# An attention stage whose SyncE transfers keep the order in which they are written, with the weights' and the noise's loads moved to later slots

## The chip, the cores and the metric

The kernel runs on one core of a Trainium2 chip. The metric is the device time of one execution, in microseconds (us). Five engines work side by side, each through its own list of instructions in order: PE (TensorE, matmuls), DVE (VectorE), ACT (ScalarE), POOL (GpSimd) and SP (SyncE, which here only issues DMAs). An engine waits where the next instruction of its list is not ready, and everything behind it waits too.

## The reference

Three stages in a row, all in float32. Attention in two steps over 4 batches, 8 heads, 576 tokens and head dimension 64: 32 packed queries per head read the keys and values, and then the tokens' own queries read the packed result. Then a mixture of 8 experts over the 2304 tokens (512 features) with noisy top-2 routing. Then a dense gated layer (2048 hidden).

```python
p_packed = sm_attn(p, k, v)                     # 32 packed rows per head
out = sm_attn(q, p_packed, p_packed)            # -> x, 2304 x 512
noisy = x @ w_gate + log1p(exp(x @ w_noise)) * noise
top2 = argpartition(-noisy, 2)[:, :2]           # softmax over the two -> top2_w
for e in range(8): out[mask] += top2_w * (relu(x[mask] @ w1[e]) @ w2[e])
h = x @ w_in;  y = (h * sigmoid(h)) @ w_out
```

## The kernel before, in words

The program has three stages: attention with routing (the first 120 us or so), the experts, and the dense layer. The change touches the first.

**Attention by slots.** A Python loop over 16 slots emits the work. Eight units of `packed` (a batch and four heads each) turn and multiply keys and values (`kp`, `s`, `a`, `pp`); ten units of `unpacked` (two tiles of 128 tokens, or one) do the second step. `START1` and `START2` say at which slot a unit starts, `LAG1` and `LAG2` when its phases follow. A unit of `unpacked` makes scores `s` (PE), a softmax over them (`mx` and `sd`: DVE, an exponential on ACT, the last multiplication on POOL, L446), turns the result (`a2p` on PE, copied to `a2T` by ACT), multiplies with `ppBD` (PE, `xp`, L460), and copies each tile to `xr` (ACT, two halves), from where SP writes it to `xs` in memory (L467). `xr` has two buffers. The last 16 columns of `xp` are the routing logits `lg`.

**Weights of expert 0.** Eight tiles of weights are loaded in the attention stage. Each takes a buffer `raw` (three of them): four DMAs of 128 KB for each of the first four tiles (L137), one DMA of 512 KB for each of the last four (L140). Two ticks of the slot loop later the tile is split into a high part (`wa0h` ... `wa7h`, one ACT activation, L115) and a low part (`wa0l` ... `wa7l`, four POOL subtractions of 256 columns, L119). The weight tiles use the same memory as keys and values: weight tile `i` waits until unit `i` of `packed` is done with its own.

**Routing.** `route` is a long chain of small DVE operations (`rt_*`). It runs once for the first 11 tiles (r0) and once for the last 7 (r1). r0 ends in a list of tokens `idx0`, by which POOL fetches two tiles `xg` (L196) for the first block of expert 0 (`hps`, `acc` with `xha`). r1 ends in `idx`, by which the rest is fetched; the second block is the first that reads `xhb`. r1 needs the last logits, so it needs the last units of `unpacked`.

**What sets the order.** A scheduler of the framework orders each engine's list by an estimate of times, free to move an instruction ahead of others that were emitted earlier; instructions given to `tc.keep_in_program_order` keep their emitted order among themselves. In the kernel before, the DMAs of the attention stage are not given to it.

Of the kernel before, what the change touches and what calls it, by code (L numbers as in the profile page):

```python
# [7 lines left out]
F32 = mybir.dt.float32  # L8
# [11 lines left out]
P = 128  # L20
B, H, S, D, PK = 4, 8, 576, 64, 32
# [4 lines left out]
REST = S - 4 * P  # L26
# [18 lines left out]
def body(ctx: ExitStack, tc: tile.TileContext, q, k, v, p, wg, wn, noise, w1, w2, w_in, w_out, out):  # L45
    nc = tc.nc
# [76 lines left out]
    def tick():  # L123

        later.append(None)
        while later.count(None) > M["delay"]:
            fn = later.pop(0)
            if fn:
                fn()

    def load(dst, src, c, eng=V, runs=False):

        hi, lo = dst
        raw = raws.tile([P, 1024], F32, name="raw", tag="raw")
# [100 lines left out]
    def expert_block(e, j0, n, x):  # L235
        ws = W[e % 2]
        acc = [None]

        def step2(f, h):
            if f == 0:  # L240
                acc[0] = [M["a"].tile([P, DM], F32, name="acc", tag="acc") for _ in range(n)]
            second(acc[0], h, ws, f, 7)
            if f == 7:
                for j, y in enumerate(acc[0]):
                    ysb = M["s"].tile([P, DM], F32, name="ysb", tag="ysb", bufs=3)
                    cp(A if j % 2 else V, ysb, y)
                    i = j0 + j
                    r0 = (e * TA + i if i < TA else E * TA + e * TB + i - TA) * P
                    nc.sync.dma_start(ys[r0:r0 + P, :], ysb)
        for f in range(8):  # L250
            ps = first(ws, x, f, n * P)
            h = relu_split(ps, n * P)
            flush(M["lag"])
            pend.append(lambda f=f, h=h: step2(f, h))
            yield f


    with ExitStack() as ax:
# [6 lines left out]
        sk = ph.enter_context(tc.tile_pool(name="attk", bufs=2))  # L265
# [143 lines left out]
        def unpacked(t, n, lg):  # L409
# [45 lines left out]
            for i in range(n):  # L455
                xr = sb.tile([P, 512], F32, name="xr")
                for g in range(2):
                    xp = pMx.tile([P, 272], F32, name="xp", tag="m")
                    for b, sl in parts:
                        T.matmul(xp[sl], aT[:, 2 * i + g, sl], ppBD[b, g], start=True, stop=True)  # L460
                    if g:
                        V.tensor_tensor(lg[:, i, :], xp[:, 256:272], lg[:, i, :], op=OP.add)
                    else:
                        V.tensor_copy(lg[:, i, :], xp[:, 256:272])
                    cp(A, runs(xr)[:, 2 * g:2 * g + 2], xp[:, 0:256].rearrange("p (b a j) -> p b a j", b=2, a=4))
                r0 = (t + i) * P
# [149 lines left out]
        for slot in range(START2[-1] + LAG2[-1] + 1):  # L616
# [339 lines left out]
```

## Time and profile before

| | us |
|---|---|
| median of 3 runs | 995.24 (993.43 to 997.77) |
| the profiled execution | 991.13 |
| its span, first to last instruction | 989.3 |
| PE busy in the span | 957.0 (97%) |
| DVE, ACT, POOL busy | 447.4, 346.4, 313.4 |

The span is that of the profiled execution; 1.8 us of its time lie outside the span. PE is busy 97% of it, so what PE lacks is in the first 150 us: the page's 40 slices (24.7 us each) show PE at 6, 9, 8, 9 and 7 tenths in the first five slices and at 9 or more from the sixth to the last but one. Below, a time at the start of a row is in us from the span's start.

### The profile page before, as it was taken

To read this page: it belongs to the slowest core of one execution; us is meant where nothing else is said; L and a number is where in the kernel's file an instruction comes from. 1 tells how busy PE (TensorE), PEld (TensorE's weight loads), DVE (VectorE), ACT (ScalarE), POOL (GpSimd) and SP (SyncE) were. 2 spreads that over 40 slices of the span, in tenths; PEclk is the share of its full clock that TensorE was granted. 3 is DMA by queue.
4 is the path that set the end of the run, shared out by engine and by line. 5 is a ranking of instruction groups with operands and counts; after the bars stand their busy time and mean duration, and the time that the engine had idled before them with its cause. 6 is when DMAs were issued, how large, how long until landed. Compare 5 with 4: busy or idle time off the path is not lost.

```text
span 989.3 us, 14385 instructions
## 1 busy us (share of the span) xinstructions
PE 957.0 (97%) x5584; PEld 821.0 (83%) x5584; DVE 447.4 (45%) x871; ACT 346.4 (35%) x631; POOL 313.4 (32%) x345
## 2 busy tenths in 40 slices
PE   6989799999999999999999999999999999999996
PEld 4767589899999999998999988888888888888884
DVE  4537763666767576766634557222122221111111
ACT  3567322433434343433323343322222222222221
POOL 2166214343525243443200136333323322222221
PEclk9989899999999999999999999999999999999998
DMA  9994324576757676566623454111011110001001
GB/s 243 249 270 161 107 65 125 188 231 202 231 167 227 188 235 199 189 226 207 188 64 117 149 194 136 54 28 37 22 53 33 32 43 1 1 1 43 0 1 46
DMA packets 82298, 122.49 MB, mean 124 GB/s; under 512 B 16432, under 2 KB 49200, under 8 KB 82224
## 3 DMA queue, kind: packets, MB, share of 16 engines
q1 hardware_dynamic: 74704, 101.58, 32.6%
q0 software_dynamic: 7520, 19.93, 7.0%
q8 instruction: 46, 0.75, 0.3%
q14 instruction: 28, 0.23, 0.1%
HBM read 93.17 MB, written 28.31 MB: 123 GB/s over the span
## 4 chain that ended last, share of the span: by engine, by line
PE 90%; DVE 4%; DMA 3%; ACT 1%; SPq 1%; issue 1%; ACTq 0%
PE hps L208 14%; PE hps L210 14%; PE hps L209 14%; PE acc L219 14%; PE acc L218 14%; PE acc L220 14%; PE xp L460 1%; PE tps L157 1%; PE s L429 1%; PE s L362 1%; DMA vm<-in_v_dram 1%; DMA km<-in_k_dram 1%; DVE rt_oa L534 1%; PE kp L351 0%; DMA raw<-wf_out 0%
## 5 line engine op out<-in xcount | busy, mean ns | idle before, releaser
L176 POOL DMA_INDIRECT xg<-xs,idx x120 | 127.0, 1059 | 195.1 <-DVE xturn L185 147.6
L750 POOL TENSOR_TENSOR gl<-sg,gh 128x512 fp32r<-128x512 f32 (+1 forms) x80 | 95.4, 1194 | 253.5 <-ACT gh L749 237.9
L231 ACT ACTIVATE hh<-hps 128x384 fp32r<-128x384 f32 (+1 forms) x128 | 56.0, 438 | 260.5 <-PE hps L210 256.8
L746 DVE TENSOR_TENSOR sg<-hps,sg 128x512 f32<-128x512 f32 (+1 forms) x80 | 50.7, 634 | 196.2 <-ACT sg L745 196.0
L232 DVE SCALAR_TENSOR_TENSOR hl<-hps,hh 128x384 fp32r<-128x384 f32 (+1 forms) x128 | 62.4, 488 | 122.0 <-ACT hh L231 121.3
L745 ACT ACTIVATE sg<-hps 128x512 f32<-128x512 f32 (+1 forms) x80 | 44.2, 553 | 189.5 <-PE hps L210 189.2
L749 ACT ACTIVATE gh<-sg 128x512 fp32r<-128x512 f32 (+1 forms) x80 | 47.1, 589 | 79.3 <-DVE sg L746 79.1
L736 POOL DMA_INDIRECT y<-ys,slots x36 | 36.7, 1019 | 110.9 <-DVE hl L232 72.4
L739 DVE TENSOR_SCALAR y<-y,gates 128x512 f32<-128x512 f32 x18 | 10.9, 607 | 37.9 <-DMA y<-ys,slots 37.9
L740 DVE SCALAR_TENSOR_TENSOR y<-y,gates,y 128x512 f32<-128x512 f32 x18 | 15.7, 871 | 25.1 <-DMA y<-ys,slots 25.0
L460 PE MATMUL xp<-ppBD,a2T 128*128 128x272 f32 (+1 forms) x80 | 23.5, 433 | 1.6 <-ACT xr L51 0.8
L185 DVE STREAM_TRANSPOSE xturn<-xg 128x512 f32<-128x512 f32 x30 | 21.2, 706 | 3.7 <-DMA wf_in<-t 2.5
L689 DVE SCALAR_TENSOR_TENSOR t<-raw,t 128x512 int32<-128x512 int32 x32 | 22.2, 693 | 0.9
L690 DVE SCALAR_TENSOR_TENSOR t<-raw,t 128x512 int32<-128x512 int32 x32 | 22.1, 691 | 0.9
L196 POOL DMA_INDIRECT xg<-xs,idx x10 | 9.7, 969 | 40.3 <-DVE idx_f L555 19.5
L686 ACT ACTIVATE t<-raw 128x512 f32<-128x512 f32 x32 | 21.2, 662 | 0.1
L208 PE MATMUL hps<-xha,wa3h 128*128 128x256 f32 (+1 forms) x56 | 17.7, 316 | 1.8 <-DVE sg L746 1.8
L160 DVE TENSOR_TENSOR xla<-tps,xha 128x512 fp32r<-128x512 f32 x14 | 9.6, 690 | 21.1 <-ACT xha L159 21.1
L53 DVE COPY ysb<-acc 128x512 f32<-128x512 f32 x24 | 16.4, 682 | 4.9 <-PE acc L220 4.8
L429 PE MATMUL s<-ppT,qT 128*128 128x64 f32 x128 | 17.9, 291 | 0.0
L208 PE MATMUL hps<-xha,wa0h 128*128 128x256 f32 (+1 forms) x56 | 17.6, 314 | 0.2 <-ACT xha L159 0.2
L208 PE MATMUL hps<-xha,wa2h 128*128 128x256 f32 (+1 forms) x56 | 17.7, 316 | 0.1
(450 smaller groups left out, 2976.4 us busy)
## 6 DMA issues: line engine op xcount, KB each, us to landing
raw<-in_moe_w_dram SPq DMA_DIRECT2D x56, 512.0 KB, 4.0
ys<-ysb SPq DMA_DIRECT2D x40, 256.0 KB, 3.7
raw<-in_moe_w_in_dram SPq DMA_DIRECT2D x16, 512.0 KB, 4.3
raw<-in_moe_w_out_dram SPq DMA_DIRECT2D x16, 512.0 KB, 4.1
xs<-xr SPq DMA_DIRECT2D x18, 256.0 KB, 2.1
km<-in_k_dram SPq DMA_DIRECT2D x8, 512.0 KB, 7.6
vm<-in_v_dram SPq DMA_DIRECT2D x8, 512.0 KB, 7.6
qm<-in_q_dram SPq DMA_DIRECT2D x8, 512.0 KB, 7.1
```

Of the source, the lines that this page charges most:

```text
L176: G.indirect_dma_start(out=xg[:, g * P:(g + 1) * P], out_offset=None, in_=xs[:, :].rearrange("n (a f) -> (n a) f", a=4), in_offset=bass.In ...
L208: T.matmul(ps, wh[:, c, s], xh[:, c, :n], start=c == 0, stop=False)
L209: T.matmul(ps, wh[:, c, s], xl[:, c, :n], start=False, stop=False)
L210: T.matmul(ps, wl[:, c, s], xh[:, c, :n], start=False, stop=c == 3)
L218: T.matmul(y, hh[:, s], wh[:, f % 2, :], start=f == 0, stop=False)
L219: T.matmul(y, hh[:, s], wl[:, f % 2, :], start=False, stop=False)
L220: T.matmul(y, hl[:, s], wh[:, f % 2, :], start=False, stop=f == last)
L231: A.activation(hh, ps, AF.Relu)
L232: V.scalar_tensor_tensor(hl, ps, 0.0, hh.bitcast(F32), op0=OP.max, op1=OP.subtract)
L746: V.tensor_tensor(sg, ps, sg, op=OP.mult)
L749: A.activation(gh, sg, AF.Copy)
L750: G.tensor_tensor(gl, sg, gh.bitcast(F32), op=OP.subtract)
```

## The change

All SyncE DMAs of the attention stage go through a helper `dma` that gives them to `tc.keep_in_program_order` as long as `M["queue"]` is set; it is cleared after the slot loop. Expert 0's weight tiles are loaded at slots 6 to 13, one a slot (before: slots 4, 5, 6, 7, 8, 8, 11 and 12), and the noise at slot 8 (before: 4). The 64-row rests of keys and values (`kr`, `vr`) have four buffers each (before three), and batch 3's value rests are loaded after its mains. The packed queries `pd` lie in one of the three `raw` buffers.

```diff
-WLOAD = 4
+WSLOT = (6, 7, 8, 9, 10, 11, 12, 13)
+NOISE = 8
...
+    def dma(dst, src):
+        ins = nc.sync.dma_start(dst, src)
+        if M["queue"]:
+            tc.keep_in_program_order(ins)
...
-                nc.sync.dma_start(raw[32 * b:32 * b + 32].rearrange("j (a f) -> j a f", a=4),
+                dma(raw[32 * b:32 * b + 32].rearrange("j (a f) -> j a f", a=4),
...
-            r = sk.tile([REST, 4, 64], F32, name=f"{nm}r", bufs=3)
+            r = sk.tile([REST, 4, 64], F32, name=f"{nm}r", bufs=4)
...
-        pd = sk.tile([P, 9, 64], F32, name="pd", bufs=1)
+        pd = raws.tile([P, 1024], F32, name="pd", tag="raw")[:, 0:576].rearrange("p (c d) -> p c d", d=64)
...
-                nc.sync.dma_start(xs[r0:r0 + P, :], xr)
+                dma(xs[r0:r0 + P, :], xr)
...
-            if slot == 4:
+            if slot == NOISE:
                 load_noise()
...
-            for i, s0 in enumerate(START1):
-                if slot == s0 + WLOAD:
+            for i, s0 in enumerate(WSLOT):
+                if slot == s0:
                     W[0].append(weight_tile(wa, "wa", i))
...
+        M["queue"] = False
```

The scheduler orders the other engines anew. Three places follow, each before and after. A number behind a name tells one tensor from another of the same name; the numbers of the two programs differ.

SP, where the first token tiles are written to `xs`, before: noise and weights stand between and ahead of the last queries (`qm`) and of the first `xs`.

```order
L302 DMA nzt<-in_moe_noise_dram 64x8
L137 DMA raw<-in_moe_w_dram 32x4x256 x5
L288 DMA qm<-in_q_dram 128x4x256
L279 DMA vr<-in_v_dram 64x4x64
L279 DMA kr<-in_k_dram 64x4x64
...
L137 DMA raw<-in_moe_w_dram 32x4x256 x7
...
L288 DMA qm<-in_q_dram 128x4x256 x2
L137 DMA raw<-in_moe_w_dram 32x4x256
L467 DMA xs<-xr 128x512
```

SP, the same place after:

```order
L108 DMA qm<-in_q_dram 128x4x256 x2
L108 DMA qr<-in_q_dram 64x8x64
L108 DMA xs<-xr 128x512 x2
L108 DMA raw<-in_moe_w_dram 32x4x256 x4
...
L108 DMA nzt<-in_moe_noise_dram 128x32
L108 DMA nzt<-in_moe_noise_dram 64x8
...
L108 DMA xs<-xr 128x512 x4
L108 DMA raw<-in_moe_w_dram 32x4x256 x4
```

The last queries are now ahead of every weight; the first weight tile stands behind the second `xs`, the second behind the fourth; the eight noise loads follow, then four `xs`, the third weight tile, three `xs` and the fourth.

ACT, the first three splits of weights before (`wa0h` to `wa2h`):

```order
L115 ACTIVATE wa0h_638<-raw_640 128x1024
L51 ACTIVATE a1T_842<-ap_835 128x512
L51 ACTIVATE ppBD11_181<-wp_809 128x16
L51 ACTIVATE xr_815<-xp_816 128x2x4x32
L51 ACTIVATE a1T_875<-ap_868 128x512
L442 ACTIVATE sd2_912<-sd2_912 128x512
L51 ACTIVATE xr_815<-xp_820 128x2x4x32
L51 ACTIVATE xr_825<-xp_826 128x2x4x32
L115 ACTIVATE wa1h_782<-raw_784 128x1024
L51 ACTIVATE qT_937<-qp_938 128x512
L51 ACTIVATE xr_825<-xp_830 128x2x4x32
L115 ACTIVATE wa2h_957<-raw_959 128x1024
```

ACT after, from the fourth token tile (`xr_987`) to `wa1h`, and from the eighth (`xr_1110`) to `wa2h`:

```order
L52 ACTIVATE xr_987<-xp_992 128x2x4x32
L52 ACTIVATE a2T2_1078<-a2p_1073 128x512
L52 ACTIVATE qT_1140<-qp_1141 128x512
L52 ACTIVATE ppBD21_189<-wp_971 128x16
L52 ACTIVATE xr_1080<-xp_1081 128x2x4x32
L52 ACTIVATE xr_1080<-xp_1085 128x2x4x32
L52 ACTIVATE qT_1140<-qp_1147 128x512
L121 ACTIVATE wa1h_1051<-raw_1053 128x1024
...
L52 ACTIVATE xr_1110<-xp_1115 128x2x4x32
...
L52 ACTIVATE a1T_1402<-ap_1395 128x512
L121 ACTIVATE wa2h_1171<-raw_1173 128x1024
```

Six ACT instructions stand between `xr_987` and `wa1h`, and six between `xr_1110` and `wa2h`; between the eleventh token tile and `wa3h` there are eight (one row of them stands for two). `wa0h` no longer stands ahead of the two `a1T`.

POOL, at the end of the attention stage, before:

```order
L119 TENSOR_TENSOR wa5l_1200<-raw_1201,wa5h_1199 128x256 x4
...
L119 TENSOR_TENSOR wa6l_1522<-raw_1523,wa6h_1521 128x256 x4
L396 COPY ppBD30_193<-px_1278 32x64 x4
L119 TENSOR_TENSOR wa7l_1614<-raw_1615,wa7h_1613 128x256 x4
L396 COPY ppBD31_197<-px_1444 32x64 x4
L446 TENSOR_TENSOR sd2_1586<-sd2_1586,mx22_1584 128x512
L196 DMA xg_1755<-xs_69,idx0_102 128x512
L196 DMA xg_1757<-xs_69,idx0_102 128x512
L446 TENSOR_TENSOR sd2_1645<-sd2_1645,mx22_1643 128x512
L446 TENSOR_TENSOR sd1_1663<-sd1_1663,mx21_1661 128x256
L196 DMA xg_2013<-xs_69,idx_101 128x512
```

POOL at the same place after; `sd2_1567`, `sd2_1631` and `sd1_1649` are what `sd2_1586`, `sd2_1645` and `sd1_1663` were, the softmax of the last three units:

```order
L125 TENSOR_TENSOR wa2l_1172<-raw_1173,wa2h_1171 128x256 x4
L411 COPY ppBD30_193<-px_1253 32x64 x4
L125 TENSOR_TENSOR wa3l_1299<-raw_1300,wa3h_1298 128x256 x4
L411 COPY ppBD31_197<-px_1426 32x64 x4
L125 TENSOR_TENSOR wa4l_1434<-raw_1435,wa4h_1433 128x256 x4
L202 DMA xg_1755<-xs_69,idx0_102 128x512
L202 DMA xg_1757<-xs_69,idx0_102 128x512
L461 TENSOR_TENSOR sd2_1567<-sd2_1567,mx22_1565 128x512
L125 TENSOR_TENSOR wa5l_1503<-raw_1504,wa5h_1502 128x256 x4
L125 TENSOR_TENSOR wa6l_1600<-raw_1601,wa6h_1599 128x256 x4
L461 TENSOR_TENSOR sd2_1631<-sd2_1631,mx22_1629 128x512
L461 TENSOR_TENSOR sd1_1649<-sd1_1649,mx21_1647 128x256
```

Behind the two fetches `xg` now stand the softmax of unit 7, two splits and the softmax of units 8 and 9, where only the latter two stood; three splits (`wa2l` to `wa4l`) stand ahead of the fetches in the stretch of r0, where two stood (`wa6l`, `wa7l`).

## Rows read from the trace of the kernel before

**Rows 1.** Stretches: length, busy PE, PEld, DVE, ACT, POOL; granted clock, DMA share, GB/s.

```profile
50.00:62.00 12.00, 9.07 (x79) 7.52 (x78) 3.90 (x13) 6.54 (x12) 5.65 (x8) 0.72 1.09 262
62.00:84.00 22.00, 21.80 (x232) 16.47 (x230) 12.29 (x37) 17.86 (x41) 16.32 (x29) 1.00 0.84 250
...
104.00:120.00 16.00, 11.05 (x77) 7.51 (x78) 11.79 (x31) 5.76 (x14) 4.25 (x5) 0.79 0.25 76
120.00:149.00 29.00, 28.31 (x227) 23.29 (x225) 17.85 (x85) 7.79 (x20) 4.76 (x5) 1.00 0.23 73
149.00:989.00 840.00, 829.07 (x4261) 723.17 (x4260) 362.15 (x550) 274.15 (x461) 261.94 (x239) 1.00 0.36 114
```

**Rows 2.** PE in order of time, 48 to 63 us: start, length; idle before, releaser.

```profile
48.46 1.10 PE L429 MATMUL s<-ppT,qT 128*128 128x64 f32 x8
...
53.57 0.66 PE L377 MATMUL ap<-ident,a 128*128 128x128 f32 x4 [2.93 <-ACT a1T L51]
...
54.52 3.47 PE L429 MATMUL s<-ppT,qT 128*128 128x64 f32 x16
```

**Rows 3.** ACT in order of time, 48 to 63 us.

```profile
51.98 1.06 ACT L115 ACTIVATE wa0h<-raw 128x1024 fp32r<-128x1024 f32 x1 [3.29 <-DMA raw<-in_moe_w_dram]
...
58.55 1.06 ACT L115 ACTIVATE wa1h<-raw 128x1024 fp32r<-128x1024 f32 x1 [2.56 <-DMA raw<-in_moe_w_dram]
```

**Rows 4.** SP in order of time, 38 to 116 us: start and length of each issue.

```profile
38.66 1.48 SPq L300 DMA_DIRECT2D nzt<-in_moe_noise_dram  x1
...
46.88 0.47 SPq L302 DMA_DIRECT2D nzt<-in_moe_noise_dram  x1
47.39 2.49 SPq L137 DMA_DIRECT2D raw<-in_moe_w_dram  x5
...
59.63 0.37 SPq L467 DMA_DIRECT2D xs<-xr  x1
...
85.46 5.10 SPq L467 DMA_DIRECT2D xs<-xr  x4
```

**Rows 5.** DMA issues of the first 125 us: KB each, median us to landing.

```profile
xs<-xr SPq DMA_DIRECT2D x18, 256.0 KB, 2.1
...
raw<-in_moe_w_dram SPq DMA_DIRECT2D x24, 128.0 KB, 3.1
```

**Rows 6.** DVE in order of time, 86 to 126 us.

```profile
91.96 0.77 DVE L487 SCALAR_TENSOR_TENSOR rt_h<-rt_h,rt_w 128x88 f32<-128x88 f32 x1
92.76 0.66 DVE L488 TENSOR_TENSOR rt_sp<-rt_sp,rt_h 128x88 f32<-128x88 f32 x1
93.45 0.67 DVE L490 COPY_PREDICATED rt_sp<-rt_big,rt_sa 128x88 f32<-128x88 int32 x1
94.16 0.25 DVE L492 TENSOR_TENSOR rt_ny<-rt_sp,nzt 128x88 f32<-128x88 f32 x1
...
98.42 0.68 DVE L439 TENSOR_REDUCE mx<-s 128x16 f32<-128x512 f32 x1
...
99.55 0.68 DVE L441 TENSOR_TENSOR sd<-s,mx 128x512 f32<-128x512 f32 x1
...
101.03 0.67 DVE L443 TENSOR_REDUCE mx<-sd 128x16 f32<-128x512 f32 x1
...
105.52 3.28 DVE L534 TENSOR_TENSOR rt_oa<-iota_lo,rt_lo 128x768 f16<-128x768 f16 x4
```

**Rows 7.** POOL in order of time, 50 to 136 us.

```profile
91.14 2.86 POOL L119 TENSOR_TENSOR wa6l<-raw,wa6h 128x256 fp32r<-128x256 f32 x4 [5.03 <-PE pp L388]
...
110.79 1.15 POOL L196 DMA_INDIRECT xg<-xs,idx  x1 [6.32 <-PE s L436]
112.25 0.95 POOL L196 DMA_INDIRECT xg<-xs,idx  x1 [0.31 <-DVE lg L464]
113.22 1.05 POOL L446 TENSOR_TENSOR sd<-sd,mx 128x512 f32<-128x512 f32 x1
114.72 0.62 POOL L446 TENSOR_TENSOR sd<-sd,mx 128x256 f32<-128x256 f32 x1 [0.44 <-DVE lg L464]
```

More of the change, by code (lines that the diff above doesn't have):

```diff
@@ L102, in body @@
     few = const.tile([P, E], F32)
-    M = {"pin": False, "w": 384, "hb": 3}
+    M = {"pin": False, "w": 384, "hb": 3, "queue": True}
+    def dma(dst, src):
+        ins = nc.sync.dma_start(dst, src)
+        if M["queue"]:
+            tc.keep_in_program_order(ins)
     def pin(ins):
@@ L136, in load @@
             for b in range(4):
-                nc.sync.dma_start(raw[32 * b:32 * b + 32].rearrange("j (a f) -> j a f", a=4),
+                dma(raw[32 * b:32 * b + 32].rearrange("j (a f) -> j a f", a=4),
                                   src[b * P:(b + 1) * P].rearrange("(a j) f -> j a f", a=4))
         else:
-            nc.sync.dma_start(raw.rearrange("p (c f) -> p c f", c=c), src.rearrange("(c p) f -> p c f", p=P))
+            dma(raw.rearrange("p (c f) -> p c f", c=c), src.rearrange("(c p) f -> p c f", p=P))
         later.append(lambda: split(hi, lo, raw, eng))
@@ L248, in step2 @@
                     r0 = (e * TA + i if i < TA else E * TA + e * TB + i - TA) * P
-                    nc.sync.dma_start(ys[r0:r0 + P, :], ysb)
+                    dma(ys[r0:r0 + P, :], ysb)
         for f in range(8):
@@ L270, in body, with load_kv, load_main, load_rest @@
         kv = {}
-        def load_kv(nm, b, g):
+        def load_kv(nm, b, g, part=2):
             src = {"k": k, "v": v}[nm]
+            if part:
+                load_main(nm, src, b, g)
+            if part != 1:
+                load_rest(nm, src, b, g)
+        def load_main(nm, src, b, g):
             m = wa.tile([P, 1024], F32, name=f"{nm}m", tag=f"wa{2 * b + g}{'hl'[nm == 'v']}")
             m = m.rearrange("p (h r) -> p h r", h=4)
-            nc.sync.dma_start(m, src[b, 4 * g:4 * g + 4, 0:512, :].rearrange("h (p r) d -> p h (r d)", r=4))
-            r = sk.tile([REST, 4, 64], F32, name=f"{nm}r", bufs=3)
-            nc.sync.dma_start(r, src[b, 4 * g:4 * g + 4, 512:576, :].rearrange("h p d -> p h d"))
-            kv[nm, b, g] = (m, r)
+            dma(m, src[b, 4 * g:4 * g + 4, 0:512, :].rearrange("h (p r) d -> p h (r d)", r=4))
+            kv[nm, b, g] = [m]
+        def load_rest(nm, src, b, g):
+            r = sk.tile([REST, 4, 64], F32, name=f"{nm}r", bufs=4)
+            dma(r, src[b, 4 * g:4 * g + 4, 512:576, :].rearrange("h p d -> p h d"))
+            kv[nm, b, g].append(r)
         qt = {}
@@ L287, in load_q @@
                 m = m[:, 0:1024].rearrange("p (h r) -> p h r", h=4)
-                nc.sync.dma_start(m, q[b, 4 * g:4 * g + 4, 0:512, :].rearrange("h (p r) d -> p h (r d)", r=4))
+                dma(m, q[b, 4 * g:4 * g + 4, 0:512, :].rearrange("h (p r) d -> p h (r d)", r=4))
                 qt["m", b, g] = m
@@ L292, in load_q @@
             o = 64 * (b % 2)
-            nc.sync.dma_start(qt["r", b // 2][o:o + 64], q[b, :, 512:576, :].rearrange("h p d -> p h d"))
+            dma(qt["r", b // 2][o:o + 64], q[b, :, 512:576, :].rearrange("h p d -> p h d"))
         nzt = one.tile([P, NT, E], F32)
@@ L299, in load_noise @@
                 t0 = 9 * (b // 2) + 4 * (b % 2)
-                nc.sync.dma_start(nzt[:, t0:t0 + 4, :],
+                dma(nzt[:, t0:t0 + 4, :],
                                   noise[b * S:b * S + 512, :].rearrange("(p r) e -> p r e", r=4))
-                nc.sync.dma_start(nzt[64 * (b % 2):64 * (b % 2) + 64, 9 * (b // 2) + 8, :],
+                dma(nzt[64 * (b % 2):64 * (b % 2) + 64, 9 * (b // 2) + 8, :],
                                   noise[b * S + 512:(b + 1) * S, :])
         load_kv("k", 0, 0)
-        pd = sk.tile([P, 9, 64], F32, name="pd", bufs=1)
-        nc.sync.dma_start(pd[:, 0:8, :], p.rearrange("b (g j) k d -> (j k) (b g) d", g=2))
+        pd = raws.tile([P, 1024], F32, name="pd", tag="raw")[:, 0:576].rearrange("p (c d) -> p c d", d=64)
+        dma(pd[:, 0:8, :], p.rearrange("b (g j) k d -> (j k) (b g) d", g=2))
         load_kv("v", 0, 0)
@@ L313, in body @@
         G.memset(wgn[64:P], 0.0)
-        nc.sync.dma_start(wgn[0:64, :, 0:8], wg.rearrange("(h d) e -> d h e", h=H))
-        nc.sync.dma_start(wgn[0:64, :, 8:16], wn.rearrange("(h d) e -> d h e", h=H))
+        dma(wgn[0:64, :, 0:8], wg.rearrange("(h d) e -> d h e", h=H))
+        dma(wgn[0:64, :, 8:16], wn.rearrange("(h d) e -> d h e", h=H))
         pT = sk.tile([P, 9, 2, P], F32, name="pT", bufs=1)
@@ L629, in body @@
                     load_kv("k", b, g)
-                    load_kv("v", b, g)
+                    load_kv("v", b, g, 1 if b == 3 else 2)
+                for g in range(2 if b == 3 else 0):
+                    load_kv("v", b, g, 0)
             for b, s0 in ((1, 0), (2, START2[1] + 1), (3, START2[3] + 1)):
```

## The prediction

> **What bounds the kernel now.** I read the stretches first. From 120 to 149 us PE is busy 28.31 of 29 us and from 149 us to the end 829.07 of 840 [rows 1]: there PE is the bound, and its order hardly changes. Whatever the attention stage gains or loses by 149 us is carried to the end whole. So the question is when PE starts that dense part, and only the first 120 us, where PE has idle time and a lower clock, matter.
>
> Then I looked for that idle time. One piece is at 50 to 54 us: PE waits 2.93 us for `a1T` [rows 2]. ACT's rows say why: `wa0h`, the split of the first weight tile, is next in ACT's list and waits 3.29 us for `raw`, which SP issued late, and `a1T` stands behind it [rows 3]. After the wait the granted clock is lower: 0.72 on average from 50 to 62 us [rows 1], and 16 matmuls of `s` take 3.47 us where 8 took 1.10 before it [rows 2]. The other piece is 104 to 120 us, where PE is busy 11.05 of 16 us at a mean clock of 0.79 [rows 1]: it waits there for the end of r0 on DVE and for the last units' `sd` on POOL.
>
> **The change part by part.** The profiled execution took 991.13 us (span 989.3, 1.8 outside), 4.1 less than the median of 995.24; I work in the profiled execution's time and add 4.1 at the end.
>
> *Gains.* (1) `wa0h` now stands behind the third and fourth token tiles, and its `raw` is issued behind the second `xs`; no weight is ahead of the last queries. The wait of 2.93 us goes; bounds 0 and 2.93, I take 2.9, since the two `a1T` are no longer behind a weight. (2) With the wait goes the slow stretch behind it: (1 - 0.72) x 12 = 3.4 us of full clock lost from 50 to 62 us [rows 1]; PE is busy nearly all of it, so I take 3.4 (bounds 0 and 3.4). (3) Unit 7's softmax stood in DVE's list inside r0: three operations of 0.68, 0.68 and 0.67 us, at 98.42, 99.55 and 101.03 [rows 6]. All but its first reduction now stand behind `rt_oa`, and that first one takes the place of unit 8's: r0 gets shorter by up to 2.0 us; I take 2.0.
>
> *Losses before r0's end.* (4) Each of the second to fourth weight tiles is now issued right behind an `xs`, and an `xs` waits for ACT's `xr`. From that `xr` to the landed tile it takes 0.37 (`xs`) [rows 4] + four issues of 2.49 / 5 = 0.50 [rows 4] + 3.1 to landing [rows 5] = 5.5 us. ACT has six, six and eight instructions before it reaches `wa1h`, `wa2h` and `wa3h`, at a mean of 17.86 / 41 = 0.44 us [rows 1]: 2.6, 2.6 and 3.5 us. So ACT stands for 2.9 + 2.9 + 2.0 = 7.8 us, and with it the `xr`, `qT` and `ppT` behind, on which PE and then DVE's logits wait. In 62 to 84 us ACT has 22 - 17.86 = 4.1 us of idle time to lose [rows 1], and PE has none. I take 7.8 - 4.1 = 3.7; bounds 0 (all of it hidden) and 7.8. (5) The noise: eight issues, 0.33 to 1.48 us each, 5.4 in sum, of which the first and last are in [rows 4], now between the second weight tile and the fifth `xs`. That `xs` lands 5.4 + 0.4 + 2.1 [rows 5] = 7.9 us after the weights' issue. `xr` has two buffers, and seven `xs` were issued from 59.63 to 85.46 us [rows 4], one per 3.7 us, so two buffers cover 7.4. I take 0.5; bounds 0 and 5.4. Before, the noise was issued from 38.66 us on, where token tiles did not yet wait for SP. (6) Three splits on POOL now lie in r0's stretch, where two lay. Beside one, three DVE operations with two inputs take 0.77, 0.66 and 0.67 us; the next, without a split, takes 0.25 [rows 6]. A split more costs 2.10 - 3 x 0.25 = 1.35 us on DVE; bounds 0 and 2.86, the length of a split [rows 7].
>
> The Trainium skill has a rule on this (SBUF — State Buffer, "Who interferes with whom"): a DVE instruction with two SBUF inputs and a GpSimd instruction that reads SBUF cannot run together; the one that comes second blocks for the whole of the other. By it the third split could hold r0 for its full 2.86 us, if a two-input operation always came next, and the sum below would be 1.5 us worse. The rows show DVE passing between the four pieces of a split at 0.66 to 0.77 us a time, and other operations running beside it, so the sum goes by the 1.35.
>
> The small edits: the fourth `kr`/`vr` buffer and the reordered rests let some transfers go earlier in the first 50 us, and `pd` gives its `raw` buffer back long before the third weight tile needs it. I take nothing for each: PE's work of the first 50 us hides them.
>
> Lead at the end of `rt_oa`: 2.9 + 3.4 + 2.0 - 3.7 - 0.5 - 1.35 = +2.75 us.
>
> *Loss behind r0.* (7) POOL's list after r0. Call R the end of `rt_oa`, 105.52 + 3.28 = 108.8 us before [rows 6]. Before, the two fetches `xg` end at 113.2 (R + 4.4) and the last `sd` at 114.72 + 0.62 = 115.3, R + 6.5 [rows 7]. Now, behind the fetches: unit 7's `sd`, 1.05 (R + 5.45). Then `wa5l`, which waits for `wa5h` on ACT; that stands behind `a2T` of unit 7, so it comes after four transposes (0.66 [rows 2]), the copy (0.44, ACT's mean) and itself (1.06 [rows 3]): R + 7.6. Then `wa5l` and `wa6l`, 2.86 each [rows 7], R + 13.3, and the `sd` of units 8 and 9, 1.05 + 0.62 [rows 7]: R + 15.0. That is 8.5 us later than before, relative to R. PE has nothing to do in between: in its list the transposes of these two `sd` stand ahead of the first block's `hps`, as before, and everything from there to 149 us is the same work at full use [rows 1]. SP is no better: the `xs` of units 8 and 9 stand behind weight tiles of expert 1 that wait for the buffers of `wa6l` and `wa7l`, and r1 needs these token tiles' copies. Bounds: 5.7 (only the two splits count, 2 x 2.86) and 10.5 (2 us more where an `xs` behind `wa7l` ends last, its landing of 2.1 [rows 5]).
>
> **Sum.** 8.5 - 2.75 = 5.75 us later: 996.9 for a profiled execution, 1001.0 against the median.
>
> **Rivals.** *No change.* ACT's waits (4) are hidden in ACT's idle time and the noise costs nothing: the lead is 2.9 + 3.4 + 2.0 - 1.35 = 6.95, against 8.5: +1.55, 996.8 against the median. For it: ACT is busy only 6.54 of 12 us from 50 to 62 [rows 1], and PE would run ahead of the weights. Against it: PE had no idle time in 62 to 84 us while ACT had 4.1, so 7.8 us can't all be hidden.
>
> *Faster.* The lead decides: the whole gain of 8.3 us stays, and the second slow stretch goes too, since POOL's and DVE's softmax of unit 7 no longer splits it up: (1 - 0.79) x 16 = 3.4 us of clock, of which PE is busy 11.05 / 16, so 2.3. The tail costs the two splits alone, 5.7. 991.1 - (8.3 + 2.3 - 5.7) = 986.2, or 990.3 against the median, the edge of faster; what ACT's other waits give back would take it below. The point from which it decides: r0 must end at 100 us or sooner. For it: the wait and the clock are in the rows, the losses (4) and (5) are worked out from a list's order. Against it: it needs (4) to (6) to cost nothing at once, and (7) is fixed by POOL's list, which holds two splits ahead of two `sd`.
>
> *Much slower.* The waits of (4) come through whole (7.8) and the lead is 2.75 - 4.1 = -1.35; with 10.5 behind r0 the shift is 11.9: 1007.1 against the median.
>
> **Chances.** Under 0.5% (5.0 us) a measurement of this kernel can't tell a difference from none; so faster is below 990.3 and slower above 1000.2. The forecast 0.45, much slower 0.12, no change 0.28, faster 0.15. The forecast's own spread reaches below 1000.2 with a small part, the no-change case above it with about as much, so: faster 0.15, same 0.29, slower 0.56. The predicted time is the forecast's, 1001. Range 990 to 1010: the low end is the faster case's own time, the high end the much slower case's 1007.1 and the 2.5 us by which the highest run (997.77) lies above the median, rounded up; below and above are left about 0.1 each.
>
> **What would show it.** (1, 2) No wait of PE for `a1T` near 50 us, clock 1.00 from 50 to 62 us. (3) `rt_oa` within 2 us less of r0's begin. (4) `wa1h`, `wa2h`, `wa3h` each with 2 to 3 us of idle time before them, released by `raw`, and PE idle for `xr` or `ppT` in the same stretch. (5) A gap before an `xr`, released by `xs`, after the noise. (6) Operations of r0 at 0.66 to 0.77 us beside three splits. (7) Two splits of 2.8 us between the fetches and the last two `sd`, and PE waiting for `sd` from POOL for several us; PE's stretch of full use, which opens with the first read of `xhb`, beginning 4 to 8 us later than at 149. The prediction is wrong if these last two `sd` end by 116 us, or if PE's dense part begins by 149 us.

## The result and the profile after

The changed kernel takes 1006.87 us (median of 5 runs, 1003.35 to 1009.57), the kernel before 995.24: a ratio of 1.0114, 95% interval 1.0086 to 1.0142. It is slower by 11.6 us; forecast were 5.75 more, 1001.0, with a range of 990 to 1010. Its profiled execution is its median (span 1004.6), while that of before lay 4.1 us under its own; so the spans differ by 15.3 us, 3.7 more than the medians, and what follows accounts for these 15.3.

The page's first line on PE and the stretches (columns as in [rows 1]):

```profile
PE 964.3 (96%) x5584; PEld 825.4 (82%) x5584; DVE 449.6 (45%) x871; ACT 347.2 (35%) x631; POOL 316.8 (32%) x345
```

```profile
50.00:62.00 12.00, 11.86 (x168) 10.06 (x167) 6.55 (x20) 7.35 (x18) 2.89 (x9) 1.00 0.51 152
62.00:84.00 22.00, 18.10 (x146) 12.77 (x145) 9.62 (x33) 11.59 (x30) 9.34 (x12) 0.93 0.44 133
...
104.00:120.00 16.00, 8.38 (x62) 7.07 (x63) 11.25 (x23) 3.38 (x7) 8.44 (x10) 0.63 0.44 154
120.00:149.00 29.00, 26.02 (x138) 18.82 (x137) 17.35 (x85) 10.70 (x25) 9.37 (x14) 0.79 0.33 106
149.00:989.00 840.00, 836.55 (x4353) 730.53 (x4352) 366.07 (x564) 276.61 (x466) 266.24 (x243) 1.00 0.36 114
```

Against [rows 1]: PE is better from 50 to 62 us (11.86 busy at 1.00, not 9.07 at 0.72), worse from 62 to 84 (18.10, not 21.80), and far worse from 104 to 149 (34.40 busy of 45 us at 0.63 and 0.79, not 39.36 at 0.79 and 1.00). The same 5584 matmuls keep PE busy 964.3 - 957.0 = 7.3 us longer, and it is idle 8.0 us longer: that is the 15.3.

PE in order of time, from the end of r0 to the first block (the answer to the stretches of [rows 1] behind 104 us):

```profile
108.40 0.38 PE L556 MATMUL ip<-rt_oc,rt_oa 128*128 128x40 f16 x6 [4.50 <-DVE rt_oa L549]
...
111.86 3.68 PE L444 MATMUL s<-ppT,qT 128*128 128x64 f32 x16 [0.28 <-DVE sd L456]
...
116.76 1.12 PE L466 MATMUL a2p<-ident,sd 128*128 128x128 f32 x4 [1.21 <-POOL sd L461]
...
126.11 1.54 PE L466 MATMUL a2p<-ident,sd 128*128 128x128 f32 x6 [1.41 <-POOL sd L461]
```

PE waits 4.50 us for `rt_oa` (1.33 before, when the scores `s` of unit 8 and the `a2p` of unit 7 stood ahead of it), comes back at the lower of its two clock levels (1.2 GHz, 0.5 of full speed), and then waits twice for `sd`. The granted clock stays there until 132 us:

```profile
108.00:120.00 12.00, 8.38 (x62) 7.07 (x63) 7.25 (x17) 2.99 (x6) 4.56 (x5) 0.51 0.53 183
120.00:132.00 12.00, 9.17 (x26) 5.86 (x25) 4.31 (x14) 6.10 (x13) 9.37 (x14) 0.50 0.55 169
```

Before, the second of these stretches has 11.99 us busy at 1.00. POOL in order of time, which answers to [rows 7]:

```profile
104.58 4.35 POOL L125 TENSOR_TENSOR wa4l<-raw,wa4h 128x256 fp32r<-128x256 f32 x4
113.21 1.16 POOL L202 DMA_INDIRECT xg<-xs,idx  x1 [4.29 <-issue]
114.67 0.95 POOL L202 DMA_INDIRECT xg<-xs,idx  x1 [0.30 <-issue]
115.64 1.07 POOL L461 TENSOR_TENSOR sd<-sd,mx 128x512 f32<-128x512 f32 x1
119.53 2.78 POOL L125 TENSOR_TENSOR wa5l<-raw,wa5h 128x256 fp32r<-128x256 f32 x4 [2.83 <-ACT wa5h L121]
122.26 2.79 POOL L125 TENSOR_TENSOR wa6l<-raw,wa6h 128x256 fp32r<-128x256 f32 x4
124.99 1.64 POOL L461 TENSOR_TENSOR sd<-sd,mx 128x512 f32<-128x512 f32 x2
```

This is the list that the prediction counted through, item by item. DVE, the operations around r0's end ([rows 6]):

```profile
94.36 0.35 DVE L406 TENSOR_SCALAR px<-pp,mx 128x128 f32<-128x128 f32 x1 [1.80 <-PE pp L403]
...
106.87 4.34 DVE L549 TENSOR_TENSOR rt_oa<-iota_lo,rt_lo 128x768 f16<-128x768 f16 x4
111.13 0.68 DVE L456 TENSOR_TENSOR sd<-s,mx 128x512 f32<-128x512 f32 x1
```

R, the end of `rt_oa`, is at 111.21 us (before 108.80). The last row is unit 7's softmax, which stood ahead of `rt_oa` and now begins behind it.

Unit 8 is late by one place too, and that on PE. Its scores `s` (16 matmuls) and the exponential of its softmax on ACT, before:

```profile
100.70 1.90 PE L429 MATMUL s<-ppT,qT 128*128 128x64 f32 x16
...
109.50 0.63 ACT L442 ACTIVATE sd<-sd 128x512 f32<-128x512 f32 x1 [3.67 <-DVE rt_rr L574]
```

The exponential after:

```profile
119.35 0.62 ACT L457 ACTIVATE sd<-sd 128x512 f32<-128x512 f32 x1
```

Before, the scores stood ahead of `ip`, the matmuls that wait for `rt_oa`, and the exponential began 0.7 us behind R. After, they stand behind `ip` (the row at 111.86), and it begins 8.1 us behind R. So the last `sd` come late on this side too, whatever POOL's list holds; e1 shows it.

The whole shift follows from four times. Below, "r0" and "r1" are the starts of their first DVE operation `rt_w`, "last sd" the end of POOL's last one, "xhb" PE's first read of it; "unit 7" says on which side of R its `sd` on POOL lies. The rows of the experiments are told further down.

| kernel | ratio | r0 | R | unit 7 | last sd | r1 | xhb |
|---|---|---|---|---|---|---|---|
| before | 1 | 89.8 | 108.8 | ahead | 115.3 = R+6.5 | 122.5 | 149.0 |
| after | 1.0114 | 90.5 | 111.2 | behind | 126.6 = R+15.4 | 136.4 | 163.4 |
| e1 | 1.0097 | 89.1 | 108.7 | behind | 121.2 = R+12.5 | 134.6 | 159.7 |
| e2 | 1.0031 | 96.9 | 117.5 | ahead | 124.0 = R+6.5 | 132.3 | 158.8 |
| e3 | 1.0080 | 89.8 | 115.1 | ahead | 125.9 = R+10.8 | 135.1 | 162.1 |
| e4 | 1.0108 | 88.0 | 109.6 | behind | 129.6 = R+20.0 | 136.2 | 164.6 |
| e5 | 1.0138 | 89.8 | 111.3 | behind | 126.8 = R+15.4 | 136.4 | 167.2 |
| e6 | 1.0084 | 91.2 | 113.2 | behind | 125.8 = R+12.5 | 142.2 | 169.4 |
| e7 | 1.0052 | 95.5 | 114.5 | ahead | 121.1 = R+6.6 | 128.2 | 156.8 |
| e8 | 1.0035 | 92.9 | 111.9 | ahead | 118.4 = R+6.5 | 126.9 | 155.4 |
| e9 | 1.0092 | 89.8 | 109.3 | behind | 118.8 = R+9.5 | 135.8 | 163.2 |
| e10 | 1.0026 | 91.2 | 110.5 | ahead | 117.1 = R+6.6 | 125.4 | 156.4 |
| e11 | 1.0126 | 91.1 | 112.8 | behind | 128.3 = R+15.4 | 137.9 | 169.0 |
| e12 | 1.0083 | 90.5 | 110.7 | behind | 123.2 = R+12.5 | 132.6 | 160.3 |

From before to after: R 2.4 later, the last `sd` 8.9 later behind R, r1 2.5 later behind that (9.7 us, before 7.2), and `xhb` 0.5 later behind r1: 14.3 of the 15.3 us. (In some traces of e5 to e11 `xhb` lies up to 31.0 us behind r1, before 26.5; why is not known, and it is not compared with the rest.)

### The profile page after: what moved, and what is told of

It reads as the page before. It is cut to its first block, busy times and chain, and to the rows that moved or that the text cites. A ratio compares the mean times of both kernels' runs of the same rounds, so it can differ in the third digit from the quotient of the medians.

```text
span 1004.6 us, 14375 instructions
## 1 busy us (share of the span) xinstructions
PE 964.3 (96%) x5584; PEld 825.4 (82%) x5584; DVE 449.6 (45%) x871; ACT 347.2 (35%) x631; POOL 316.8 (32%) x345
## 4 chain that ended last, share of the span: by engine, by line
PE 87%; DMA 4%; SPq 3%; DVE 2%; ACT 2%; POOL 1%; issue 1%; ACTq 0%; POOLq 0%; DVEq 0%
PE hps L214 14%; PE hps L215 14%; PE hps L216 14%; PE acc L224 14%; PE acc L225 14%; PE acc L226 13%; SPq L108 3%; DMA raw<-in_moe_w_dram 2%; PE tps L163 1%; PE s L377 1%; PE xp L475 1%; PE s L444 1%; DMA kr<-in_k_dram 1%; POOL y L754 1%; DMA y<-ys,slots 1%
## 5 line engine op out<-in xcount | busy, mean ns | idle before, releaser
L475 PE MATMUL xp<-ppBD,a2T 128*128 128x272 f32 (+1 forms) x80 | 25.9, 463 | 4.8 <-ACT xr L52 4.2
L475 PEld LDWEIGHTS xp<-ppBD,a2T 128*128 128x128 f32 (+1 forms) x80 | 12.8, 203 | 11.2 <-ACT xr L52 8.5
L411 POOL COPY ppBD<-px 32x64 f32<-32x64 f32 x32 | 8.4, 262 | 32.6 <-DVE px L406 24.0
L214 PE MATMUL hps<-xhb,wa0h 128*128 128x384 f32 (+1 forms) x48 | 17.1, 356 | 1.5 <-DVE xla L166 1.5
```

What stands on the lines that cost most here:

```text
L214: T.matmul(ps, wh[:, c, s], xh[:, c, :n], start=c == 0, stop=False)
```

## The experiments

The theory after the result: the order on SP costs little by itself; what costs is that POOL's list holds splits of weights and unit 7's late `sd` between the fetches and the last two `sd`. The rivals: the noise's place, SP with its token tiles behind weights, the low clock. e5 to e8 and e9 to e11 ran on two other chips, on which the kernel before takes 1004.5 and 1005.3 us, so kernels are compared by their ratios to the kernel before on the same chip.

**e1: POOL's last `sd` (second piece of the diff) and splits (first piece) kept in written order.**

```diff
+            if eng is G and keep:
+                tc.keep_in_program_order(ins)
...
+            if M["late"]:
+                tc.keep_in_program_order(ins)
...
+            if slot == 13:
+                M["late"] = True
```

> The changed kernel, but from slot 13 on POOL's softmax multiplications and the splits of the last weight tiles keep the order in which they are written: behind the two fetches stand the softmax of units 7, 8 and 9 and only then the splits wa4l to wa7l. Theory (the splits ahead of the last softmax, on POOL's list, are the main loss): the last softmax ends about 7 us after rt_oa instead of 15.4, r1 begins 6 to 9 us earlier, 997 to 1001 us. Rival (the pinned SP queue is the main loss; POOL's order only hides it): the token tiles behind expert 1's weights on SP still come late, r1 begins at most 3 us earlier, 1003 to 1006 us.

1005.32 us, ratio 1.0097 (1.0065 to 1.0129). POOL in order of time:

```profile
110.76 1.15 POOL L204 DMA_INDIRECT xg<-xs,idx  x1 [6.72 <-issue]
...
113.23 1.04 POOL L463 TENSOR_TENSOR sd<-sd,mx 128x512 f32<-128x512 f32 x1
119.10 1.05 POOL L463 TENSOR_TENSOR sd<-sd,mx 128x512 f32<-128x512 f32 x1 [4.83 <-ACT sd L459]
120.58 0.61 POOL L463 TENSOR_TENSOR sd<-sd,mx 128x256 f32<-128x256 f32 x1 [0.43 <-DVE mx L462]
121.15 2.77 POOL L125 TENSOR_TENSOR wa4l<-raw,wa4h 128x256 fp32r<-128x256 f32 x4
```

No split stands in the tail, and the last `sd` still ends at R + 12.5. Unit 8's `sd` waits 4.83 us for its exponential on ACT (at 116.91), which stands behind `a2T` of unit 7 and `wa5h`; `a2T` waits for unit 7's `sd`, 113.23. Unit 8's scores, too, begin only at 109.33, behind `ip`, and take 3.68 us. So the splits are worth 15.4 - 12.5 = 2.9 us of the tail, and the other 6.0 belong to units 7 and 8 behind R, with the clock in them (e9). The theory's time is missed, and the rival's numbers come: r1 only 1.8 us earlier than after the change. Whether the order on SP is the reason, as the rival has it, e5 and e6 ask.

**e2: no order on SP, all else as changed. e3: the order, with the old slots for weights and noise.**

```diff
 e2
-    M = {..., "queue": True}
+    M = {..., "queue": False}
 e3
-WSLOT = (6, 7, 8, 9, 10, 11, 12, 13)
-NOISE = 8
+WSLOT = (4, 5, 6, 7, 8, 8, 11, 12)
+NOISE = 4
```

> The changed kernel with the new slots of weights and noise, the fourth rest buffer and pd in a raw buffer, but no DMA is given to keep_in_program_order. Theory (pinning puts weights behind token tiles on SP, and by that their splits behind r0 on POOL): the splits wa5l to wa7l stand ahead of the fetches again, the last softmax ends 6 to 7 us after rt_oa, 990 to 998 us. Rival (the later slots of weights and noise cost the time by themselves): 1002 to 1007 us.

> The changed kernel with the weights at their old slots (4, 5, 6, 7, 8, 8, 11, 12) and the noise at its old slot 4; the pinned order stays. Theory: on POOL one split (wa6l) stands ahead of the fetches and one (wa7l) between them and the last softmax, so the tail costs about 3 us in place of 8.9, while the pinned queue still holds up the first token tiles: 997 to 1002 us. Rival (pinning alone costs it all): 1005 to 1008 us. Rival (the slots alone cost it): 993 to 997 us.

e2: 997.75 us, 1.0031 (1.0013 to 1.0049), as the theory has it. e3: 1004.37, 1.0080 (1.0053 to 1.0107), nearer to the rival, by which the order costs by itself. With the new slots the order is worth 1.0114 / 1.0031 = 1.008. In e2's profiled execution, the longest of its ten, r0 begins 7.1 us later than before, but its tail is short: unit 7's `sd` lies ahead of the fetches again, and no split behind them.

```profile
111.53 1.05 POOL L461 TENSOR_TENSOR sd<-sd,mx 128x512 f32<-128x512 f32 x1 [5.25 <-DVE rt_lo L538]
119.47 1.16 POOL L202 DMA_INDIRECT xg<-xs,idx  x1 [6.89 <-PE s L451]
...
121.91 1.06 POOL L461 TENSOR_TENSOR sd<-sd,mx 128x512 f32<-128x512 f32 x1
123.41 0.62 POOL L461 TENSOR_TENSOR sd<-sd,mx 128x256 f32<-128x256 f32 x1 [0.44 <-DVE lg L479]
```

In e3 unit 7's `sd` lies ahead of R, but `wa6l` and `wa7l` stand in the tail (R + 10.8; kernels with unit 7 ahead and no split there have R + 6.5), and r0 lasts 25.3 us.

**e4: two buffers for `qr`.** After the change SP stands from 47.88 to 55.47 us at a `qr`, whose single buffer PE reads until 55.44, and the first token tiles stand behind it (SP's rows are in the next section).

```profile
54.84 0.60 PE L437 MATMUL qp<-ident,qr 128*128 128x128 f32 x4
```

```diff
-name="qr", bufs=1
+name="qr", bufs=2
```

> The changed kernel with two buffers for the queries' rest rows qr in place of one. In the changed kernel SP stands from 47.9 to 55.5 us at the third batch's qr, which waits for PE, and the first token tiles' xs are queued behind it; ACT then waits 3.5 us for xs and PE 1.75 us for xr. Theory (this head-of-line wait costs 2 to 4 us before r0): the first xs goes 3 us earlier or more, no wait of ACT for xs near 61 us, 1003 to 1005 us. Rival (off the path, since r0 waits for later tiles): no change, 1006 to 1008 us.

1007.29 us, 1.0108 (1.0076 to 1.0140). r0 begins 2.5 us sooner, and all of it is lost: the scheduler now puts `wa7l` between the last two `sd` as well (R + 20.0). The rival's time comes, but not its reason: r0 did begin sooner.

**e5: SP freed behind r0: expert 1's first weights are issued behind the last token tile (the flag is cleared behind expert 0's second block, no longer behind the slot loop; the stores `ys` stay free). e6: e1 and e5 together.**

```diff
-                    dma(ys[r0:r0 + P, :], ysb)
+                    nc.sync.dma_start(ys[r0:r0 + P, :], ysb)
...
-        M["queue"] = False
...
+                M["queue"] = False
```

> The changed kernel, but expert 1's first weight loads keep their written order too, so on SP the last five token tiles' xs stand ahead of them (in the changed kernel xs of units 8 and 9 stand behind weight tiles that wait for the buffers of wa5l to wa7l). POOL's order is that of the changed kernel. Theory (two holds in parallel, POOL's order and SP's order; freeing one leaves the other): last softmax at 126 to 127 us as in the changed kernel, r1 begins at 134 to 136 us, 1004 to 1007 us. Rival (SP alone holds r1): r1 begins at 130 us or sooner, 999 to 1003 us.

> Both: POOL's last softmax ahead of the splits wa4l to wa7l, and the last token tiles ahead of expert 1's weights on SP. Theory (two holds in parallel): last softmax at 121 us as with POOL's order alone, but r1 begins at 128 to 130 us in place of 134.6, 998 to 1001 us. Rival (neither; it is the low clock behind r0): r1 at 133 us or later, 1003 to 1006 us.

e5: ratio 1.0138 (1.0091 to 1.0185), last `sd` and r1 as after, as the theory has it: SP alone isn't it. e6: 1.0084 (1.0048 to 1.0121), with runs from 1009.4 to 1021.0 us; its profiled execution is the longest of them. It has its last `sd` at R + 12.5 as e1, and r1 at 142.2, not at the 128 to 130 expected. ACT says why:

```profile
132.65 1.06 ACT L121 ACTIVATE wa7h<-raw 128x1024 fp32r<-128x1024 f32 x1 [3.41 <-DMA raw<-in_moe_w_dram]
133.62 0.64 ACT L52 ACTIVATE xr<-xp 128x256 f32<-128x256 f32 x2
```

and PE behind it:

```profile
134.04 2.18 PE L479 MATMUL xp<-ppBD,a2T 128*128 128x272 f32 x4 [2.34 <-ACT xr L52]
```

With three `raw` buffers, the eighth tile can be loaded only when the split `wa4l` is done, which the pinned POOL does behind the last `sd`; `wa7h` waits for it, and two `xr` stand behind `wa7h`. On SP this load stands ahead of the last five token tiles and holds the queue until 128.90 us, so in e6 SP isn't free either. e1 has the wait of `wa7h` too (1.63 us).

**e7: the order for keys, values and queries alone, free from slot 6 on.**

```diff
+            if slot == 6:
+                M["queue"] = False
```

> The changed kernel with the order kept only for the loads of keys, values and queries (up to slot 6); weights, noise and token tiles are free to move. Theory (the loss comes from keeping weights, noise and xs in one order): the splits stand ahead of the fetches on POOL again, last softmax 6 to 8 us after rt_oa, 994 to 999 us, as without any pinning (997.75). Rival (keeping the queries ahead of the weights is the loss): 1003 us or more.

1.0052 (1.0029 to 1.0074), nearer to the theory (994 to 999 us are ratios of 0.999 to 1.004) than to the rival (1.008 or more). So keeping weights, noise and token tiles in order is worth 1.0114 / 1.0052 = 1.006. The tail is short (R + 6.6), and r1 is the earliest of all kernels with a pinned order; but weights and noise overtake queries again, and r0 begins 5.7 us later than before. PE's longest wait up to 175 us:

```profile
PE qp L437 <- DMA qm<-in_q_dram: 6.1, 1, 6.1
```

**e8: the kernel before, noise loaded at slot 8. e11: the changed kernel, noise at slot 4.**

```diff
 e8
-            if slot == 4:
+            if slot == 8:
                 load_noise()
 e11
-NOISE = 8
+NOISE = 4
```

> The kernel before with one edit: the noise is loaded at slot 8 in place of 4; nothing is pinned. On SP the first three weight tiles move ahead of the noise. Theory (gain 1 and 2 of the prediction are real and can be had alone): wa0h finds its raw landed, PE's wait of 2.93 us for a1T goes and the slow stretch from 54 to 61 us with it, 990 to 993 us. Rival (the weights now delay the keys and queries that follow, and PE waits for these): 995 to 999 us.

> The changed kernel with the noise at slot 4 again; all the rest as changed. On SP the eight noise loads leave the place between the second weight tile and the fifth xs. Theory (the noise costs 0.5 us by the prediction's working, and what is gained before r0 can be lost behind it): the wait of 1.4 us of ACT for xs near 79 us goes, ratio 1.008 to 1.012, no clear difference from 1.0114. Rival (the noise's place is a main cost): ratio 1.006 or less.

e8: 1.0035 (1.0011 to 1.0059), the rival's numbers. PE's wait for `a1T` is gone, and PE waits for other things in the same place, 4.6 us in four waits from 51 to 61 us, the longest two:

```profile
51.10 1.18 PE L460 MATMUL xp<-ppBD,a2T 128*128 128x272 f32 x4 [1.20 <-ACT a2T L51]
...
58.70 0.63 PE L422 MATMUL qp<-ident,qm 128*128 128x128 f32 x4 [1.38 <-DMA qm<-in_q_dram]
```

e11: 1.0126 (1.0067 to 1.0185), with after's tail, R + 15.4. The noise's place is no main cost.

**e9: e1 with eight more matmuls (overwritten at once) ahead of `ip`. e10: the kernel before with six.** They give PE work while it waits for `rt_oa`.

```diff
+            ipf = pMx.tile([P, 272], F32, name="ip", tag="m")
+            for _ in range(8 if t0 == 0 else 0):
+                T.matmul(ipf, ident, ppBD[0, 0], start=True, stop=True)
```

> The first experiment's kernel (the changed kernel with POOL's last softmax ahead of the splits), with eight matmuls of 128x272 more, whose result is overwritten, in PE's list ahead of r0's matmuls ip, where PE waited 2.8 us for rt_oa. The orders of POOL and SP are as there (but for one piece of a weight tile). Theory (the clock, 0.5 from 108 to 124 us there, follows PE's wait for rt_oa and is a good part of the loss): with the wait filled, the granted clock stays at 1.0 for more of 106 to 124 us, the first read of xhb comes 2 to 4 us earlier (159.7 there), ratio to the kernel before 1.005 to 1.008. Rival (the low clock costs nothing here, since PE waits for other engines anyway): clock higher but xhb no earlier than 1 us, ratio 1.009 to 1.011.

> The kernel before with six such matmuls ahead of r0's a2p and ip, where PE waited 1.94 and 1.33 us, and nothing else changed; its slow stretch from 105.8 to 112.6 us is worth 3.4 us of full clock, of which PE was busy some 70%. Theory: the slow stretch goes or shrinks, 1 to 3 us faster than the kernel before, ratio 0.997 to 0.999. Rival (PE waits for DVE's rt_oa and POOL's sd in this stretch anyway): ratio 0.999 to 1.002.

e9: 1.0092 (1.0063 to 1.0121), against e1's 1.0097. Stretches of e1, then of e9:

```profile
108.00:120.00 12.00, 9.30 (x53) 7.30 (x53) 7.07 (x23) 4.98 (x9) 4.04 (x4) 0.50 0.46 153
120.00:132.00 12.00, 10.01 (x49) 7.88 (x48) 3.04 (x11) 5.35 (x12) 11.57 (x18) 0.83 0.55 158
```

```profile
108.00:120.00 12.00, 9.25 (x74) 7.56 (x74) 7.91 (x24) 5.11 (x10) 5.96 (x7) 0.72 0.44 153
120.00:132.00 12.00, 9.15 (x41) 7.21 (x41) 2.57 (x9) 5.24 (x12) 9.85 (x15) 0.78 0.68 216
```

The low stretch begins some 4 us later, but the clock falls again behind a wait for `xr`, from 128 us on; over both stretches (0.72 + 0.78 - 0.50 - 0.83) x 12 = 2.0 us of full clock are given back. The last `sd` comes at R + 9.5, 3.0 sooner, and not by the clock alone: unit 8's scores take 2.00 us in place of 3.68, and its exponential now stands ahead of `wa5h` and `a2T` on ACT.

```profile
109.99 2.00 PE L446 MATMUL s<-ppT,qT 128*128 128x64 f32 x16
...
113.61 0.63 ACT L459 ACTIVATE sd<-sd 128x512 f32<-128x512 f32 x1 [2.68 <-DVE sd L458]
```

It begins at R + 4.3 (e1: R + 8.2). But r1 begins no sooner, as the rival has it: `wa7h` waits 3.47 us for `raw`, and PE's `xp` behind it 2.32 us. e10: 1.0026 (0.9989 to 1.0062), no difference shown; the low stretch moves, and isn't gone.

**e12: e1 with a buffer of its own for the eighth weight tile** (`M["rp"]` is the pool from which its `raw` is taken).

```diff
+                    if i == 7:
+                        M["rp"] = one
```

> The kernel of e1 (POOL's last softmax and splits kept in program order), with a landing buffer of its own for expert 0's eighth weight tile. In e1's trace, wa7h on ACT waits 1.63 us for raw, whose buffer the split wa4l on POOL gives back only at 123.9 us, and the xr behind it hold PE's last xp; in e6, where SP is free, the same wait is 3.41 us. Theory: the splits that the pinned list puts late on POOL hold r1, in the changed kernel directly, in e1 by way of the buffer, wa7h and xr. Then wa7h no longer waits, the last sd still ends some 12 us behind rt_oa, and r1 begins 7 to 9 us behind that sd, as in the kernel before (7.2): near 129 instead of 134.6 us in e1; ratio 1.003 to 1.006. Rival: the low clock, or SP with its token tiles behind expert 1's weights, holds r1 by itself: wa7h's wait goes, and r1 still begins at 132 us or later; ratio 1.008 to 1.011.

1003.13 us, 1.0083 (1.0064 to 1.0103). ACT in order of time:

```profile
121.21 1.05 ACT L121 ACTIVATE wa7h<-raw 128x1024 fp32r<-128x1024 f32 x1
...
131.37 0.38 ACT L52 ACTIVATE xr<-xp 128x256 f32<-128x256 f32 x1 [2.58 <-DMA xs<-xr]
```

`wa7h` waits no more, and r1 begins 2.0 us sooner than in e1, not the 5.6 that the theory wanted: now an `xr` waits 2.58 us for its token tile, which stands on SP behind weights. The rival's numbers hold. But R came 2.0 us later in this execution; counted from the last `sd`, r1 is at 9.4 us (e1: 13.4), close to the 7 to 9 that the theory named. So three covers lie over one stretch: POOL's `sd`, the `raw` buffer with `wa7h`, and SP's order. e1 took away a part of the first, e12 the second with it, e5 the third alone, and each time r1 was held by what was left. All three at once were not tried. Of the kernels that keep weights and token tiles in one order, none is clear of the changed one (1.0086 to 1.0142); e2 and e7, which free them, are, and that shows the cause. How the loss is shared among the covers is argued from traces. No version beats the kernel before.

## Why the prediction was right, point by point, and where its size failed

Slower was right, and the time lies in the range; the size was half of what came. That the range reached so far is luck in part: its high end is the much slower case, whose cause did not come.

**(1, 2) Right in place.** No wait for `a1T` is left, and the clock from 50 to 62 us is 1.00. But r0 begins 0.65 us later than before, so the 6.3 us were spent again by 90 us: from 62 to 84 us PE is idle for 3.9 us, before for 0.2; see (4). e8, where this wait goes by another edit, gains nothing by it either: other waits stand in its place.

**(3) Failed: the step "r0 gets shorter by up to 2.0 us".** Unit 7's operations did leave r0, but r0 lasts 20.7 us, before 19.0. DVE waits 1.80 us for `pp` in their place, and (6) adds 1.6. And they were not gone, only moved behind R, where they have a part in the 6.0 us of e1.

**(4) Waits right, size too high; the cause of the delay missed.** ACT, [rows 3] after the change:

```profile
64.81 0.66 ACT L52 ACTIVATE xr<-xp 128x256 f32<-128x256 f32 x2 [3.50 <-DMA xs<-xr]
...
74.53 1.06 ACT L121 ACTIVATE wa1h<-raw 128x1024 fp32r<-128x1024 f32 x1 [1.70 <-DMA raw<-in_moe_w_dram]
...
79.16 0.38 ACT L52 ACTIVATE xr<-xp 128x256 f32<-128x256 f32 x1 [1.41 <-DMA xs<-xr]
...
91.21 1.06 ACT L121 ACTIVATE wa2h<-raw 128x1024 fp32r<-128x1024 f32 x1 [1.38 <-DMA raw<-in_moe_w_dram]
...
98.33 1.06 ACT L121 ACTIVATE wa3h<-raw 128x1024 fp32r<-128x1024 f32 x1 [1.29 <-DMA raw<-in_moe_w_dram]
```

The three waits for `raw` are 1.70, 1.38 and 1.29, 4.4 in sum, not 7.8. The longest wait is one that the prediction hasn't: 3.50 us for `xs` at 64.81. And PE stands from 62 to 84 us behind `xs`, not behind `raw`: it waits for `xr` once 1.75 us and once, at 79.60, 1.32.

```profile
65.24 0.73 PE L475 MATMUL xp<-ppBD,a2T 128*128 128x272 f32 x2 [1.75 <-ACT xr L52]
```

SP ([rows 4]) says where the first of these waits comes from:

```profile
46.21 1.67 SPq L108 DMA_DIRECT2D qm<-in_q_dram  x2
55.47 0.61 SPq L108 DMA_DIRECT2D qr<-in_q_dram  x1
...
58.04 1.04 SPq L108 DMA_DIRECT2D xs<-xr  x2
```

SP stands 7.6 us at `qr`, whose only buffer is in use, and the first `xs`, pinned behind it, wait as well; issued right behind the queries, one of the `xs` takes 6.7 us to land (2.4 in the median of the ten from 50 to 90 us). The prediction asked what a pinned weight waits for, and did not ask it of the last queries. e4 prices it: r0 2.5 us sooner.

**(5) Right.** 0.5 was taken; one wait of ACT for `xs`, 1.41 us, follows the noise. In e11 the noise is elsewhere and this wait gone, but PE still waits 1.10 us for `xr` in the same place, and the time is no better.

**(6) Right.** `rt_oa` takes 4.34 us beside `wa4l`, 3.28 without a split [rows 6], and `rt_up` 0.69 in place of 0.17: 1.6 lost, 1.35 taken. `wa4l` gets longer as well (4.35, other splits 2.78). Both are four instructions each. A piece of `wa4l` runs from 106.78 to 107.54; the first piece of `rt_oa` begins at 106.87 and takes 1.48 us (a quarter of 3.28 is 0.82), the next of `wa4l` 1.43 (a quarter of 2.78 is 0.70), the second of `rt_oa` 1.48 again: they take turns. The rule weighed in the prediction (the Trainium skill, SBUF — State Buffer, "Who interferes with whom") says that the later of the two blocks for the whole of the other; read for one piece against one piece, the trace agrees.

**Lead.** Forecast +2.75 us, measured -2.4: this is the step of the sum that was mis-sized, by 5.2 us. Of these, 2.75 lie ahead of r0 (it begins 0.65 us late, forecast 2.1 early), where e4 prices the unseen wait at `qr` at 2.5; the other 2.4 lie inside r0, by (3) and (6) (1.76 us longer, forecast 0.65 shorter).

**(7) Total right, its parts not.** R + 15.4, forecast R + 15.0; the tail grew 8.9 us, forecast 8.5: POOL's list ran as counted. But the lower bound called the two splits 5.7 us of that, and without them only 2.9 go (e1). The other 6.0 were not seen as a loss of their own. The prediction let PE have nothing to do in between; there PE runs unit 8's scores, which had moved behind `ip`, so the last `sd` could not have come at R + 6.5 without the splits. The total was right for the list as it stood; that the splits were the loss in it was not. The sign that it named, `xhb` 4 to 8 us later than at 149, was passed: 14.4.

**Missing from the sum: the clock.** PE's wait for `rt_oa` grew from 1.33 to 4.50 us, since the work of units 7 and 8 no longer stands ahead of it, and the low clock behind it lasts to 132 us. From the last `sd` to r1 2.5 us more pass than before. Four `xp` take 2.18 us there (before 1.08) and eight `tps` 1.92 (before 1.04), so an estimate from these rows puts 2.0 of the 2.5 down to the clock. How much of the 15.3 us is the clock's own stays open: in e9, where 2.0 us of clock are given back, the time does not move, but there r1 is held by `wa7h` as well.

**Rivals.** "No change" (996.8) and "faster" (990.3) fell with the lead. The measured 1006.87 is the time of "much slower" (1007.1), and its two terms are near: a lead of -1.35 (measured -2.4) and 10.5 behind r0 (measured 8.9, and 2.5 more to r1). Its cause isn't: it lets the waits of (4) come through whole, and these were 4.4 us. The match is luck.

## What to carry to other kernels

Fixing one queue's order lets a scheduler rearrange every other engine: count what each list, PE's too, then holds between the last producer and the first consumer, for 8.9 of the 15.3 us were lost there. An operation that leaves a critical stretch must be priced where it arrives, with what has moved along with it; here unit 7's softmax, and with it unit 8's scores, arrived behind r0, where 6.0 us were lost without any split (e1), and gave nothing in front. In a pinned queue every transfer, not only the moved one, needs the question which buffer it waits for.

## What was not expected of the hardware

One wait of 4.50 us was followed by 24 us at the lower level of the clock (0.51 and 0.50 of full speed from 108 to 132 us), in which PE was busy 17.6 us and its longest single waits were 1.0 to 1.4 us; before, behind a wait of 1.94 us for `sd` and one of 1.33, the clock from 104 us on was 0.72, 0.50, 0.93 and 1.00 in four steps of 4 us. A set of 16 `s` matmuls takes 3.68 us in it; in e9, at the full clock, 2.00.
